# Values as weights in batch 0, and heads 2 to 7 of the second attention block ordered behind the first MoE's start

## The chip, the cores and the metric

The kernel runs on one core of a Trainium2 chip. The metric is the device time of one execution in microseconds (us), as a median over executions. The profile is one such execution taken by the hardware profiler. Engines: TensorE (PE; its weight loads are shown apart as PEld), VectorE (DVE), ScalarE (ACT), GpSimd (POOL), and SyncE (SP), which issues most DMAs.

## What is computed

An attention with decay (4 batches, 8 heads, 576 positions, 64 elements a head), whose output, 2304 tokens of 512, goes through two MoE layers:

```python
scores = scale * np.matmul(q, k.transpose(0, 1, 3, 2))
cum = np.cumsum(np.log(np.clip(f, 0.0001, 1.0)), axis=-1)
decay = cum[:, :, :, None] - cum[:, :, None, :]
scores = np.where(causal, -1000000000.0, scores + decay)
attn = np.exp(scores - np.max(scores, axis=-1, keepdims=True))
attn = attn / (np.sum(attn, axis=-1, keepdims=True) + 1e-09)
x = heads_side_by_side(np.matmul(attn, v))         # [2304, 512]
h = x @ w_in                                       # 512 -> 2048
x = np.maximum(0.01 * h, h) @ w_out                # -> 512
out = ((x @ w_a) * (x @ w_b)) @ w_out2             # 512 -> 1536 -> 512
```

## The kernel before

**The MoE layers** hold most of the work. A MoE operand is kept as a high and a low part (`xh`, `xl`; the same for weights), and each product is done three times: high by high, high by low, low by high. The weights come from DRAM as doubles, 512 KB twice per weight tile, and are turned into the two parts by four VectorE operations in `from_double` (L95, L96, L97, L100), one more for the low part (L88), and two on ScalarE. There are 16 such tiles in the first MoE. Its first stage, `l1` (L594), takes a chunk of 256 tokens and a pair of weight tiles and makes 24 products (L606) into the PSUM tile `h`; `l2` (L621) makes the second stage (products at L633, tile `y`).

**The attention** goes by blocks (b, r): batch b, and r = 0 for queries 0 to 255, r = 1 for 256 to 575. The 64 last queries of a batch are handled apart (`att_last`). Block (0,0) gives chunk 0 of the tokens, which the first MoE products need, and block (0,1) gives chunk 1. Within a block, heads go in pairs, and each head passes through two generators:

- `att_scores` (L192): loads queries and keys, transposes them on TensorE (`tq`, `tk`, in batch 0), makes the mask with the decay on GpSimd into `p` (from the broadcast `cumb`, L336 and L363), the scores on TensorE (`s`), adds and takes the minimum on VectorE (L346), and exponentials on ScalarE with their row sums (`stat`). In batch 0 the scores of both heads of a pair are computed side by side, in the two row halves of the array. In the other batches `p` is then multiplied by the reciprocal of its row sum on ScalarE (L353 to L356).
- `att_values` (L403): transposes `p` (tile `pp`), copies it to SBUF (`ph`), and multiplies by the values. In batch 0 a block of `ph` (128 keys by 128 queries) is the weight and 64 columns of values stream through it, so the result `av` has queries on partitions; VectorE multiplies it by the reciprocal sums (`rec`, `xn`), two transposes (`px`) bring it to the layout of x, and `evac` (L398) splits it: ScalarE copies the high part, VectorE subtracts for the low part.

In block (0,0) `av` and `px` use the PSUM bank with tag `h`, which `l1` uses also. Mask tiles have the tags `p0` and `p1` with two buffers each, so a mask for a later head waits until an earlier `p` has been transposed.

**What sets the order.** The program is written as generators that are interleaved; a planner then simulates the program and orders the instructions of each engine by priority, with an offset of 300 for the attention's engines (class `Ahead`, `pe_att` and its like). The engines run the order as planned. In the main part (L800 on), the attention of batch 0's block (0,0) is issued with a weight tile loaded every nine steps, the first two `l1`/`l2` items of chunk 0 get a priority offset of 2000, and then block (0,1) runs among the remaining items of chunk 0, and items of chunk 1 follow.

Of the kernel before, what the change touches and what calls it, by code (L numbers as in the profile page):

```python
# [8 lines left out]
F32 = mybir.dt.float32  # L9
# [4 lines left out]
ALU = mybir.AluOpType  # L14
# [3 lines left out]
P = 128  # L18
# [8 lines left out]
def kernel(  # L27
# [13 lines left out]
    nc = tc.nc  # L41
# [23 lines left out]
    class Ahead:  # L65
# [5 lines left out]
        def __getattr__(self, name):  # L71
# [5 lines left out]

            return call if self.offset else method

    pe_att, act_att, dve_att, pool_att = (Ahead(e) for e in (nc.tensor, nc.scalar, nc.vector, nc.gpsimd))  # L80

    def f32(ap):
        return ap.bitcast(F32)
# [107 lines left out]

    def att_scores(b, r, h, st):  # L192

        hp, j = h // 2, h % 2
        bh = b * H + h
        a = j * 64
# [127 lines left out]
        for i in range(2):  # L324
# [25 lines left out]
            yield  # L350
            exp(pt, s)
            yield
        if b:  # L353
            rec = over(2 * j, 2)
            for i in range(2):
                act_att.mul(ps[i], ps[i], rec[:, i : i + 1])  # L356
            yield
        if r == 1:
            if j == 0:
                p4s[b, hp] = ap_.tile([P, S], F32, tag="p4", name=f"p4_{nm}")  # L360
# [36 lines left out]

    def evac(hi, lo, src):  # L398
        act_att.copy(hi, src)
        dve_att.tensor_tensor(out=lo, in0=src, in1=f32(hi), op=ALU.subtract)  # L400


    def att_values(b, r, h, st):  # L403
# [44 lines left out]
        for z, (tiles, hi) in enumerate(parts):  # L448
            pp = ps_a.tile([P, 4, P], F32, tag="ps", bufs=3, name=f"pp_{nm}_{z}")
            for m, (kt, i) in enumerate(tiles):  # L450
                pe_att.transpose(pp[:, m, :], ps[i][:, kt * P : kt * P + P], ident)
            if b == 0:
                act_att.copy(hi, pp[:, : len(tiles), :])
            else:
                lo = pl[:, : 3 + z, z, :] if r else pl.rearrange("p a b c -> p (a b) c")[:, 0:3, :]
                evac(hi, lo, pp[:, : len(tiles), :])
            yield
# [4 lines left out]
        if b == 0:  # L462
            if j == 0:
                return

            rec = ap_.tile([P, 4], F32, tag="rec", bufs=3, name=f"rec_{nm}")
            dve_att.tensor_scalar(rec, stats[pair][:, 1, 0:4], 1e-9, None, op0=ALU.add)
            dve_att.reciprocal(rec, rec)
            if r == 0:
                av = ps_y.tile([P, 2, 2, 64], F32, tag="h", bufs=1, name=f"av_{nm}")  # L470
            else:
                av = ps_a.tile([P, 2, 2, 64], F32, tag="ps", bufs=3, name=f"av_{nm}")
            for u in range(2):
                for i in range(2):
                    nt = 2 * r + i + 1
                    for kt in range(nt):
                        pe_att.matmul(av[:, u, i, :], phs[u][:, at[kt, i], :], vhl[:, kt, u, :], start=(kt == 0), stop=(kt == nt - 1))
            xs = ap_.tile([P, 2, 2, 64], F32, tag="xn", bufs=1, name=f"xn_{nm}")
            for u in range(2):
                over_u = rec[:, 2 * u : 2 * u + 2].rearrange("p (i o) -> p i o", o=1).to_broadcast([P, 2, 64])  # L480
                dve_att.tensor_tensor(out=xs[:, :, u, :], in0=av[:, u, :, :], in1=over_u, op=ALU.mult)
            yield
            if r == 0:
                px = ps_y.tile([P, T1], F32, tag="h", bufs=1, name=f"px_{nm}")
            else:
                px = ps_a.tile([P, T1], F32, tag="ps", bufs=3, name=f"px_{nm}")
            for i in range(2):
                pe_att.transpose(px[:, i * P : i * P + P], xs[:, i, :, :].rearrange("p u d -> p (u d)"), ident)
            ch, cl = x_chunk(tok0 // T1)
            evac(ch[:, hp, :], cl[:, hp, :], px)  # L490
            yield
            return
        av = ps_a.tile([P, 256], F32, tag="ps", bufs=3, name=f"av_{nm}")
# [101 lines left out]
    def l1(i, pr):  # L595
        ch, cl = x_chunk(i)
        last = i >= NB1 - 2
        hps = (pools["ps_ab"] if last else ps_y).tile(
            [P, 2, T1], F32, tag="ab0" if last else "h", bufs=2 if last else 1, name=f"h_{i}_{pr}"
        )  # L600
        for u in range(2):
            wih, wil = wa[2 * pr + u][0], wa[2 * pr + u][1]
            n = 0
            for c in reversed(range(ND)):
                for w, x in ((wih, ch), (wih, cl), (wil, ch)):
                    nc.tensor.matmul(  # L606
                        hps[:, u, :], w[:, c * P : c * P + P], x[:, c, :], start=(n == 0), stop=(n == 3 * ND - 1)
                    )
                    n += 1

        hs = mp.tile([P, 2, T1], F32, tag="hs", name=f"hs_{i}_{pr}")
        gh = mp.tile([P, 2, T1], F32R, tag="gh", name=f"gh_{i}_{pr}")
        gl = mp.tile([P, 2, T1], F32R, tag="gl", name=f"gl_{i}_{pr}")
        with tc.high_priority(offset=1):
            nc.scalar.activation(gh, hps, AF.Prelu, alpha=0.01)  # L615
            nc.scalar.activation(hs, hps, AF.Prelu, alpha=0.01)  # L616
        with tc.high_priority(offset=400 if last else 0):
            nc.vector.tensor_tensor(out=gl, in0=hs, in1=f32(gh), op=ALU.subtract)  # L618
        return gh, gl
# [290 lines left out]
```

## Time and profile before

| | us |
|---|---|
| median of 3 runs | 1097.92 (1096.82 to 1098.43) |
| the profiled execution | 1095.32 |
| its span | 1093.5 |
| PE busy in the span | 1064.4 (97%) |
| DVE, ACT, POOL busy | 589.3, 534.6, 216.0 |

The profiled execution has 1.8 us outside its span. On the page, a chain of what ended last is made up of PE for 88%, DVE for 6% and DMA for 3%. Its slices show that DMA is heavily used in the first 60 us and that the clock granted to TensorE is at full speed in nearly all slices.

How to read it: a row of a timeline has the start, the time from there to the end of the last of its records, the engine, the line, the operation, output and inputs by the program's names, shape and count. TensorE's records overlap and their ends are modelled, so what a step takes there is read from start to next start. The line is L76 for all that goes through the class `Ahead`, so such rows are told apart by their names.

### The profile page before, as it was taken

The numbers are of one execution on the slowest core, as the hardware profiler recorded it, in microseconds if no ns is written. First come the engines' busy times: TensorE is split into PE (matmuls) and PEld (weight loads), VectorE is DVE, ScalarE is ACT, GpSimd is POOL, SyncE is SP. The second block draws the span as 40 slices with busy tenths as digits, with TensorE's granted clock in tenths as the row PEclk, the third lists the DMA queues.
The fourth block names the chain that finished last, engine by engine and source line by source line (L and its number), as shares of the span: only waits on it lengthen the run. The fifth ranks groups of instructions, "written<-read, shape, count | busy, mean of one in ns | idle before, by whom it ended". The sixth has DMA issues, their size and how long they took to land.

```text
span 1093.5 us, 19240 instructions
## 1 busy us (share of the span) xinstructions
PE 1064.4 (97%) x7021; PEld 962.3 (88%) x7021; DVE 589.3 (54%) x1314; ACT 534.6 (49%) x1189; POOL 216.0 (20%) x434
## 2 busy tenths in 40 slices
PE   3899999999999999999999999999999999999998
PEld 2678899999999999999999998888888888888897
DVE  5989847868778887577348888212111211211122
ACT  5666658887778788778435554212112111211121
POOL 3834423334233423332000000102002000100000
PEclk9999999999999999999999999999999999999999
DMA  8986135332452435421126562102000100100010
GB/s 234 263 241 185 37 61 110 83 77 61 78 118 62 99 66 98 95 52 43 53 70 206 180 220 82 40 1 77 1 1 25 43 1 1 49 1 1 1 39 21
DMA packets 185727, 86.76 MB, mean 79 GB/s; under 512 B 143840, under 2 KB 173536, under 8 KB 185632
## 3 DMA queue, kind: packets, MB, share of 16 engines
q1 hardware_dynamic: 180736, 80.80, 28.4%
q10 hardware_dynamic: 4896, 4.72, 1.3%
q8 instruction: 56, 0.92, 0.3%
q14 instruction: 39, 0.32, 0.1%
HBM read 75.96 MB, written 9.51 MB: 78 GB/s over the span
## 4 chain that ended last, share of the span: by engine, by line
PE 88%; DVE 6%; DMA 3%; ACT 1%; issue 1%; SPq 1%; POOL 0%; DVEq 0%; POOLq 0%; ACTq 0%
PE ab L702 27%; PE y L633 17%; PE h L606 17%; PE o L725 13%; PE av L76 5%; PE s L76 5%; PE pp L76 3%; DVE w_a L88 1%; DMA raw_a<-in_moe_w_out_dram 1%; DVE c_a L100 1%; DVE c_a L97 1%; DVE c_a L95 1%; DMA cumb<-cum_dram 1%; DVE c_a L96 0%; DVE p L346 0%
## 5 line engine op out<-in xcount | busy, mean ns | idle before, releaser
L702 PE MATMUL ab<-yh,w_ab 128*128 128x512 f32 (+1 forms) x960 | 279.6, 367 | 0.0
L633 PE MATMUL y<-gh,w_a 128*128 128x256 f32 x1152 | 224.8, 282 | 0.0
L606 PE MATMUL h<-xh,w_a 128*128 128x256 f32 x1152 | 224.2, 282 | 0.0
L702 PEld LDWEIGHTS ab<-yh,w_ab 128*128 128x128 f32 x960 | 174.3, 188 | 30.2
L708 DVE TENSOR_TENSOR p<-ab,p 128x512 f32<-128x512 f32 (+1 forms) x60 | 38.3, 638 | 285.1 <-PE ab L702 285.1
L606 PEld LDWEIGHTS h<-xh,w_a 128*128 128x128 f32 x1152 | 183.8, 189 | 3.1 <-issue 1.9
L633 PEld LDWEIGHTS y<-gh,w_a 128*128 128x128 f32 x1152 | 183.3, 188 | 1.0 <-ACT gh L615 0.2
L702 PE MATMUL ab<-yl,w_ab 128*128 128x512 f32 (+1 forms) x480 | 176.4, 367 | 0.0
L606 PE MATMUL h<-xl,w_a 128*128 128x256 f32 x576 | 163.2, 283 | 0.0
L633 PE MATMUL y<-gl,w_a 128*128 128x256 f32 x576 | 161.5, 282 | 0.0
L725 PE MATMUL o<-w_c,pph 128*128 128x512 f32 x432 | 142.6, 390 | 0.0
L707 ACT COPY p<-ab 128x512 f32<-128x512 f32 (+1 forms) x60 | 32.7, 544 | 173.7 <-PE ab L702 173.6
L633 PEld LDWEIGHTS y<-gl,w_a 128*128 128x128 f32 x576 | 108.7, 189 | 2.3 <-issue 1.3
L606 PEld LDWEIGHTS h<-xl,w_a 128*128 128x128 f32 x576 | 108.8, 189 | 1.6 <-issue 1.2
L702 PEld LDWEIGHTS ab<-yl,w_ab 128*128 128x128 f32 x480 | 90.2, 188 | 15.4
L336 POOL TENSOR_SCALAR p<-cumb,ncum_t 128x384 f32<-128x384 f32 (+1 forms) x112 | 77.3, 698 | 128.4 <-PE pp L76 50.4
L87 ACT CAST pph<-p 128x512 fp32r<-128x512 f32 (+1 forms) x60 | 34.7, 578 | 127.6 <-DVE p L708 127.6
L88 POOL TENSOR_TENSOR yl<-sy,yh 128x512 fp32r<-128x512 f32 (+1 forms) x16 | 19.9, 1253 | 389.3 <-ACT yh L87 389.2
L725 PEld LDWEIGHTS o<-w_c,pph 128*128 128x128 f32 x432 | 81.2, 188 | 16.5
L314 ACT ACTIVATE p<-p,stat 128x384 f32<-128x384 f32 (+4 forms) x128 | 76.9, 602 | 37.4 <-DVE stat L346 29.9
L725 PE MATMUL o<-w_c,ppl 128*128 128x512 f32 x216 | 84.3, 390 | 0.0
L618 DVE TENSOR_TENSOR gl<-hs,gh 128x512 fp32r<-128x512 f32 x72 | 51.0, 708 | 41.3 <-ACT hs L616 41.0
(140 smaller groups left out, 1730.9 us busy)
## 6 DMA issues: line engine op xcount, KB each, us to landing
cumb<-cum_dram SPq DMA_DIRECT2D x32, 288.0 KB, 3.8
raw_a<-in_moe_w_in_dram SPq DMA_DIRECT2D x16, 512.0 KB, 4.5
raw_a<-in_moe_w_out_dram SPq DMA_DIRECT2D x16, 512.0 KB, 5.4
raw_ab<-in_moe_w_a_dram SPq DMA_DIRECT2D x12, 512.0 KB, 4.9
raw_ab<-in_moe_w_b_dram SPq DMA_DIRECT2D x12, 512.0 KB, 6.7
raw_c<-in_moe_w_out_dram SPq DMA_DIRECT2D x12, 512.0 KB, 5.9
xq<-in_q_dram SPq DMA_DIRECT2D x144, 32.0 KB, 2.0
y_dram<-yo ACTq DMA_DIRECT2D x18, 256.0 KB, 3.0
```

The costliest lines, as they stand in the source:

```text
L76: return method(*args, **kw)
L87: nc.scalar.copy(hi, src)
L88: (lo_engine or nc.gpsimd).tensor_tensor(out=lo, in0=src, in1=f32(hi), op=ALU.subtract)
L314: act_att.activation(pt, pt, AF.Exp, bias=stat[:, 0, s : s + 1], scale=-1.0, accum_out=stat[:, 1, s : s + 1])
L336: pool_att.tensor_scalar(pt, cumb[:, :n], 1.0, ncum_t[:, t, bh : bh + 1], op0=ALU.mult, op1=ALU.add)
L606: nc.tensor.matmul(hps[:, u, :], w[:, c * P : c * P + P], x[:, c, :], start=(n == 0), stop=(n == 3 * ND - 1))
L618: nc.vector.tensor_tensor(out=gl, in0=hs, in1=f32(gh), op=ALU.subtract)
L633: nc.tensor.matmul(o, w[:, d * P : d * P + P], g[:, u, :], start=(fi == 0 and n == 0 and d % 2 == 0), stop=(fi == NF1 - 1 and n == 2 and d ...
L702: nc.tensor.matmul(o[:, :tn], w[:, c * P : c * P + P], y[:, c, :tn], start=(m == 0), stop=(m == 3 * ND - 1))
L707: nc.scalar.copy(p[:, :tn], ab[0][:, :tn])
L708: nc.vector.tensor_tensor(out=p[:, :tn], in0=ab[1][:, :tn], in1=p[:, :tn], op=ALU.mult)
L725: nc.tensor.matmul(o, g[:, t * P : t * P + P], w, start=(fi == 0 and m == 0), stop=(fi == NF2 - 1 and m == 2))
```

## The change

**Values as weights.** In batch 0, `p` is now multiplied by the reciprocal of its row sum on ScalarE, as in the other batches, by a `rec` for each head. The values of a head (128 keys by 64 elements) are then the weight, and the probabilities stream through it, 256 columns at a time (128 in the last key tile). The two heads of a pair write PSUM partitions 0 to 63 and 64 to 127 of one tile, that is, they use the two column halves of the array; the first product of the pair waits for the copy of the second head's `ph`. The result is in the layout of x as it is, so the multiplication and the transposes `px` go, and `evac` reads `av`. For a pair of block (0,1), 14 products of 64 columns become 6 of 256 and 2 of 128; in block (0,0), 6 become 2 and 2.

**The order.** A class `Behind` adds to each TensorE and VectorE instruction of `att_scores` for heads 2 to 7 of block (0,1) a dependence that is for order alone. On TensorE it stands behind the first `l1` item's 24th product, on VectorE behind the last low part of chunk 0.

```diff
+    class Behind:
+        def __init__(self, engine):
+            self.engine, self.first = engine, None
+        def __getattr__(self, name):
+            method = getattr(self.engine, name)
+            def call(*args, **kw):
+                made = method(*args, **kw)
+                tc.add_manual_dep(made.ins, self.first.ins.name, ORDER, reason="second block behind the first MoE's start")
+                return made
+            return call
+    ORDER = mybir.DependencyInfo(mybir.DependencyClass.NoSync, mybir.DependencyReason.DATA)
...
+    pe_free, dve_free = pe_att, dve_att
+    pe_held, dve_held = Behind(pe_free), Behind(dve_free)
+    def engines_of(b, r, h):
+        return (pe_held, dve_held) if (b, r) == (0, 1) and h >= 2 else (pe_free, dve_free)
...
     def att_scores(b, r, h, st):
+        pe_att, dve_att = engines_of(b, r, h)
...
-        if b:
-            rec = over(2 * j, 2)
-            for i in range(2):
-                act_att.mul(ps[i], ps[i], rec[:, i : i + 1])
-            yield
+        rec = over(2 * j, 2)
+        for i in range(2):
+            act_att.mul(ps[i], ps[i], rec[:, i : i + 1])
+        yield
...
-                act_att.copy(hi, pp[:, : len(tiles), :])
+                st["second"] = act_att.copy(hi, pp[:, : len(tiles), :])
...
-            rec = ap_.tile([P, 4], F32, tag="rec", bufs=3, name=f"rec_{nm}")
-            dve_att.tensor_scalar(rec, stats[pair][:, 1, 0:4], 1e-9, None, op0=ALU.add)
-            dve_att.reciprocal(rec, rec)
...
-            for u in range(2):
-                for i in range(2):
-                    nt = 2 * r + i + 1
-                    for kt in range(nt):
-                        pe_att.matmul(av[:, u, i, :], phs[u][:, at[kt, i], :], vhl[:, kt, u, :], start=(kt == 0), stop=(kt == nt - 1))
-            xs = ap_.tile([P, 2, 2, 64], F32, tag="xn", bufs=1, name=f"xn_{nm}")
-            for u in range(2):
-                over_u = rec[:, 2 * u : 2 * u + 2].rearrange("p (i o) -> p i o", o=1).to_broadcast([P, 2, 64])
-                dve_att.tensor_tensor(out=xs[:, :, u, :], in0=av[:, u, :, :], in1=over_u, op=ALU.mult)
...
-            for i in range(2):
-                pe_att.transpose(px[:, i * P : i * P + P], xs[:, i, :, :].rearrange("p u d -> p (u d)"), ident)
-            ch, cl = x_chunk(tok0 // T1)
-            evac(ch[:, hp, :], cl[:, hp, :], px)
+            nkt = 2 * r + 2
+            for kt in range(nkt):
+                i0 = 1 if kt == nkt - 1 else 0
+                a0 = at[kt, i0]
+                for u in range(2):
+                    made = pe_att.matmul(
+                        av[u * 64 : u * 64 + 64, i0 * P : 256], vhl[:, kt, u, :], phs[u][:, a0 : a0 + 2 - i0, :],
+                        start=(kt == 0), stop=(kt == nkt - 1),
+                    )
+                    if kt == u == 0:
+                        tc.add_manual_dep(made.ins, st["second"].ins.name, SYNC, reason="both heads at once")
+            ch, cl = x_chunk(tok0 // T1)
+            low = evac(ch[:, hp, :], cl[:, hp, :], av)
+            if r == 0:
+                dve_held.first = low
...
+                    if pe_held.first is None and u == 1 and n == 3 * ND - 1:
+                        pe_held.first = made
```

The places where the order changes are shown in three pieces. In the names, a zero for batch 0 is left out at the front: `p_1_0_2` is the mask of block (0,1), head 0, query tile 2; `p_0_6` is head 6 of block (0,0); `h_0` is the first MoE's first pair of weight tiles for chunk 0. The line numbers after the change are 18 to 24 higher.

TensorE just ahead of the first MoE product, before:

```order
L76 MATMUL pp_1_0_0_846<-ident,p_1_0_2_655 128x128 x3
L76 MATMUL px_0_7_531<-ident,xn_0_7_516 128x128 x2
L76 MATMUL tq_1_4_864<-ident,xq_1_4_854 128x128 x2
L76 MATMUL tq_1_4_864<-ident,xk_1_4_855 128x64
L76 MATMUL tk_1_4_0_869<-ident,xk_1_4_855 128x128 x2
L76 MATMUL tk_1_4_2_873<-ident,xk_1_4_855 128x128 x2
L76 MATMUL tk_1_4_2_873<-ident,xk_1_4_855 128x64
L76 MATMUL s_0_1_0_0_738<-kn_1_0_626,qn_1_0_625 64x288
L76 MATMUL s_0_1_0_0_738<-kn_1_0_626,qn_1_0_625 128x288
L76 MATMUL pp_1_0_1_883<-ident,p_1_0_3_703 128x128 x4
L76 MATMUL pp_1_1_0_900<-ident,p_1_1_2_664 128x128 x3
L606 MATMUL h_0_536<-xh_290,w_a_199 128x256
```

And after:

```order
L76 MATMUL av_0_7_525<-ph_0_6_501,vn_0_6_498 64x256
L76 MATMUL av_0_7_525<-ph_0_7_519,vn_0_6_498 64x256
L76 MATMUL av_0_7_525<-ph_0_6_501,vn_0_6_498 64x128
L76 MATMUL av_0_7_525<-ph_0_7_519,vn_0_6_498 64x128
L76 MATMUL tk_1_0_2_642<-ident,xk_1_0_624 128x128 x2
L76 MATMUL tk_1_0_2_642<-ident,xk_1_0_624 128x64
L76 MATMUL s_1_0_2_656<-kn_1_0_622,qn_1_0_621 128x384 x2
L624 MATMUL h_0_532<-xh_288,w_a_195 128x256
L624 MATMUL h_0_532<-xl_289,w_a_195 128x256
```

The transposes `px` are gone, and the transposes of heads 2 to 5, the 512 and 288 scores of heads 0 and 1 and the transposes of their probabilities stand behind the first MoE item.

VectorE up to the last low part of chunk 0 (`xl`), before:

```order
L76 TENSOR_TENSOR xn_0_7_516<-av_0_7_509,rec_0_7_506 128x2x64 x2
L96 TENSOR_SCALAR c_a_720<-c_a_720 128x1024
L88 TENSOR_TENSOR w_a_525<-c_a_519,w_a_525 128x1024
L97 SCALAR_TENSOR_TENSOR c_a_720<-raw_a_482,c_a_720 128x1024
L95 TENSOR_SCALAR c_a_778<-c_a_778 128x1024
L346 ISA p_1_0_3_703,stat_1_0_624<-s_1_0_3_708,p_1_0_3_703 128x512
L346 ISA stat_1_0_624 128x1
L346 ISA p_1_1_3_712,stat_1_0_624<-s_1_0_3_708,p_1_1_3_712 128x512
L346 ISA stat_1_0_624 128x1
L100 SCALAR_TENSOR_TENSOR c_a_720<-raw_a_482,c_a_720 128x1024
L96 TENSOR_SCALAR c_a_778<-c_a_778 128x1024
L76 TENSOR_TENSOR xl_291<-px_0_7_531,xh_290 128x256
```

And after:

```order
L76 TENSOR_TENSOR xl_289<-av_0_5_480,xh_288 128x256
L124 SCALAR_TENSOR_TENSOR c_a_462<-raw_a_377,c_a_462 128x1024
L119 TENSOR_SCALAR c_a_507<-c_a_507 128x1024
L120 TENSOR_SCALAR c_a_507<-c_a_507 128x1024
L112 TENSOR_TENSOR w_a_468<-c_a_462,w_a_468 128x1024
L121 SCALAR_TENSOR_TENSOR c_a_507<-raw_a_428,c_a_507 128x1024
L76 TENSOR_TENSOR xl_289<-av_0_7_525,xh_288 128x256
L371 ISA p_1_0_2_651,stat_1_0_620<-s_1_0_2_656,p_1_0_2_651 128x384
L371 ISA stat_1_0_620 128x1
```

Eight weight steps (41 before the last low part, 33 after), the scores of heads 0 and 1 of block (0,1) and the multiplications `xn` no longer stand ahead of it.

GpSimd at the last masks of block (0,0), before:

```order
L76 AFFINE_SELECT p_0_6_402<-p_0_6_402 128x128
L76 TENSOR_SCALAR p_0_7_414<-cumb_0_6_346,ncum_t 128x128
L76 TENSOR_SCALAR p_0_7_414<-cumb_0_6_346,ncum_t 128x256
L76 AFFINE_SELECT p_0_6_402<-p_0_6_402 128x128
L363 TENSOR_SCALAR p_0_1_0_732<-cumb_1_0_651,ncum_t_71 64x576
L76 AFFINE_SELECT p_0_7_414<-p_0_7_414 128x128 x2
L367 AFFINE_SELECT p_0_1_0_732<-p_0_1_0_732 64x64
```

And after:

```order
L76 TENSOR_SCALAR p_0_6_410<-cumb_0_6_355,ncum_t 128x256
L387 TENSOR_SCALAR p_0_1_0_738<-cumb_1_0_647,ncum_t_71 64x576
L76 AFFINE_SELECT p_0_6_410<-p_0_6_410 128x128
L76 TENSOR_SCALAR p_0_7_434<-cumb_0_6_355,ncum_t 128x128
L76 TENSOR_SCALAR p_0_7_434<-cumb_0_6_355,ncum_t 128x256
L76 AFFINE_SELECT p_0_6_410<-p_0_6_410 128x128
L391 AFFINE_SELECT p_0_1_0_738<-p_0_1_0_738 64x64
```

The first mask row of block (0,1) (64 rows for the last queries, from `cumb_1_0`) has moved from behind both masks of head 7 and the selects of head 6 to a place ahead of them.

## Rows read from the trace of the kernel before

**Rows 1.** Page: busy us (share of the span) x instructions, by engine.
```profile
PE 1064.4 (97%) x7021; PEld 962.3 (88%) x7021; DVE 589.3 (54%) x1314; ACT 534.6 (49%) x1189; POOL 216.0 (20%) x434
```
**Rows 2.** Stretches: us, PE, PEld, DVE, ACT, POOL busy (x), PEclk, DMA, GB/s.
```profile
0.00:70.00 70.00, 46.62 (x185) 32.21 (x186) 56.43 (x111) 42.44 (x90) 35.66 (x55) 0.98 0.88 255
70.00:160.00 90.00, 89.18 (x669) 76.68 (x668) 71.77 (x162) 57.21 (x124) 34.10 (x48) 1.00 0.43 108
67.00:70.00 3.00, 3.00 (x14) 2.79 (x14) 3.00 (x5) 2.17 (x4) 1.49 (x1) 0.50 0.98 334
```
**Rows 3.** Timeline of DVE: start, us, operation, [idle before it, its releaser].
```profile
60.07 0.49 DVE L76 TENSOR_TENSOR xn<-av,rec 128x128 f32<-128x128 f32 x2 [1.97 <-PE av L76]
...
64.34 0.67 DVE L346 CUSTOM_DVE_ANT_0 p<-s,p 128x512 f32<-128x512 f32 x1
...
65.56 1.22 DVE L100 SCALAR_TENSOR_TENSOR c_a<-raw_a,c_a 128x1024 int32<-128x1024 int32 x1
66.69 0.68 DVE L96 TENSOR_SCALAR c_a<-c_a 128x1024 int32<-128x1024 int32 x1
67.30 0.41 DVE L76 TENSOR_TENSOR xl<-px,xh 128x256 fp32r<-128x256 f32 x1
...
124.98 1.28 DVE L88 TENSOR_TENSOR w_a<-c_a,w_a 128x1024 fp32r<-128x1024 f32 x1 [1.17 <-ACT w_a L87]
```
**Rows 4.** Timeline of PE around the first MoE item.
```profile
68.62 0.56 PE L606 MATMUL h<-xh,w_a 128*128 128x256 f32 x1
68.98 0.41 PE L606 MATMUL h<-xl,w_a 128*128 128x256 f32 x1
69.19 0.63 PE L606 MATMUL h<-xh,w_a 128*128 128x256 f32 x2
...
72.29 1.38 PE L76 MATMUL s<-kn,qn 64*64 64x288 f32 x4
73.59 0.44 PE L76 MATMUL pp<-ident,p 128*128 128x128 f32 x2
```
**Rows 5.** Timeline of PE: last weight pair of chunk 0, values, first product of chunk 1.
```profile
146.16 0.28 PE L606 MATMUL h<-xh,w_a 128*128 128x256 f32 x1
146.27 0.28 PE L606 MATMUL h<-xl,w_a 128*128 128x256 f32 x1
...
146.91 3.29 PE L76 MATMUL av<-vn,ph 128*128 128x64 f32 x28
150.01 0.37 PE L76 MATMUL s<-ks,qhh 128*128 128x256 f32 x1
...
157.30 0.28 PE L606 MATMUL h<-xh,w_a 128*128 128x256 f32 x1
```
**Rows 6.** Timeline of PE: scores of both heads of a pair.
```profile
79.01 0.92 PE L76 MATMUL s<-kn,qn 64*128 64x384 f32 x4
...
86.71 1.13 PE L76 MATMUL s<-kn,qn 64*128 64x512 f32 x4 [0.34 <-DVE stat L346]
87.77 0.50 PE L606 MATMUL h<-xh,w_a 128*128 128x256 f32 x2
...
103.27 0.92 PE L76 MATMUL s<-kn,qn 64*128 64x384 f32 x4
104.12 0.39 PE L633 MATMUL y<-gl,w_a 128*128 128x256 f32 x1
```
**Rows 7.** Timeline of PE: the two transposes of one pair's result.
```profile
89.63 0.38 PE L76 MATMUL px<-ident,xn 128*128 128x128 f32 x2
89.84 0.71 PE L76 MATMUL pp<-ident,p 128*128 128x128 f32 x5
```
**Rows 8.** Groups on ACT by form, 0 to 200 us: busy, mean ns | idle before.
```profile
L356 ACT ACTIVATE p<-p,rec 128x256 f32<-128x256 f32 x8 | 4.0, 498 | 0.0
L356 ACT ACTIVATE p<-p,rec 128x128 f32<-128x128 f32 x8 | 3.2, 398 | 3.5 <-DVE rec L320 3.5
```
**Rows 9.** Timeline of POOL: a mask row of block (0,1).
```profile
41.66 1.28 POOL L363 TENSOR_SCALAR p<-cumb,ncum_t 64x576 f32<-64x576 f32 x1 [1.48 <-DMA cumb<-cum_dram]
```

More of the change, by code (lines that the diff above doesn't have):

```diff
@@ L399, in evac @@
         act_att.copy(hi, src)
-        dve_att.tensor_tensor(out=lo, in0=src, in1=f32(hi), op=ALU.subtract)
+        return dve_att.tensor_tensor(out=lo, in0=src, in1=f32(hi), op=ALU.subtract)
     def att_values(b, r, h, st):
@@ L464, in att_values @@
                 return
-            rec = ap_.tile([P, 4], F32, tag="rec", bufs=3, name=f"rec_{nm}")
-            dve_att.tensor_scalar(rec, stats[pair][:, 1, 0:4], 1e-9, None, op0=ALU.add)
-            dve_att.reciprocal(rec, rec)
             if r == 0:
-                av = ps_y.tile([P, 2, 2, 64], F32, tag="h", bufs=1, name=f"av_{nm}")
+                av = ps_y.tile([P, T1], F32, tag="h", bufs=1, name=f"av_{nm}")
             else:
-                av = ps_a.tile([P, 2, 2, 64], F32, tag="ps", bufs=3, name=f"av_{nm}")
@@ L482, in att_values @@
-            yield
-            if r == 0:
-                px = ps_y.tile([P, T1], F32, tag="h", bufs=1, name=f"px_{nm}")
-            else:
-                px = ps_a.tile([P, T1], F32, tag="ps", bufs=3, name=f"px_{nm}")
-            for i in range(2):
-                pe_att.transpose(px[:, i * P : i * P + P], xs[:, i, :, :].rearrange("p u d -> p (u d)"), ident)
-            ch, cl = x_chunk(tok0 // T1)
-            evac(ch[:, hp, :], cl[:, hp, :], px)
+                av = ps_a.tile([P, T1], F32, tag="ps", bufs=3, name=f"av_{nm}")
@@ L605, in l1 @@
                 for w, x in ((wih, ch), (wih, cl), (wil, ch)):
-                    nc.tensor.matmul(
+                    made = nc.tensor.matmul(
                         hps[:, u, :], w[:, c * P : c * P + P], x[:, c, :], start=(n == 0), stop=(n == 3 * ND - 1)
                     )
+                    if pe_held.first is None and u == 1 and n == 3 * ND - 1:
+                        pe_held.first = made
                     n += 1
```

## The prediction, made blind

> **What bounds the kernel now.** I read the busy table of the page first, then the busy times and the granted clock by stretch, then the timelines of VectorE and TensorE around the first MoE. TensorE is busy for 97% of the span [rows 1], but not evenly: 46.62 of the first 70 us against 89.18 of the 90 us after them, and nothing of the change reaches beyond 160 us except by moving the rest earlier [rows 2]. So two things are worth time: the first MoE product comes sooner, or TensorE gets less to do once it is full. Time taken from another engine after 70 us is worth nothing by itself.
>
> What sets the first product is VectorE, busy in nearly all of the time up to 70 us. The last low part of the first chunk of x starts at 67.30; ahead of it VectorE waits 1.97 us for the values product of block (0,0), and converts weights that are needed much later [rows 3]. The first MoE product starts at 68.62, 1.32 us behind that low part [rows 4]. The weights themselves are no limit there: the last of the sixteen is ready at 126.3 and is wanted first at 146.16, a slack of 20 us [rows 3, 5].
>
> **Part 1: values as weights.** Per pair of heads in block (0,1) the old form takes 3.10 us for the values (146.91 to 150.01, 28 records) and 0.21 for the two transposes of the result, 3.31 together [rows 5, 7]. The new form has four passes per pair, three of 256 columns and one of 128, each with both heads in column halves. No row of before shows column halves. The nearest are score pairs, two heads at once in row halves: 0.85 us for 384 columns (103.27 to 104.12), 1.06 for 512 (86.71 to 87.77), so 1.64 ns a column and 0.22 beside the columns [rows 6]. By these a pass of 256 costs 0.64 and one of 128 costs 0.43, 2.35 a pair; if all of the 0.22 hides, as the weight loads of whole-array products do (a new weight every 0.11 us [rows 5]), it is 1.47. Below that I see nothing, since the columns have to stream. I take the middle, 1.9, being between a shape that is like it and a load pattern that is like it: 1.4 saved a pair, 5.6 for four pairs, with 3.8 and 7.4 as ends. In block (0,0) the same edit saves time on an engine that is idle for a third of that stretch [rows 2], so nothing there.
>
> A rule speaks against the better end. The Trainium skill, "TensorE: Matmul & The Clock Gate", Part 3 (What overlaps and what doesn't), says that a weight load runs beside a product in flight only where their row groups differ; column halves share all rows, so by it every load would be bare, and the pair would cost the 2.35. The rows of whole-array products do not agree as they stand (a load for each product, and none of it is seen), so I don't go all the way to that end; by the rule the total below would be 1092.9 in place of 1091.1.
>
> What is added for it: two scalings of the probabilities per head on ScalarE. Like shapes take 0.398 us for 128 columns and 0.498 for 256 [rows 8], 0.78 ns a column, so 0.60 and 0.70 for 384 and 512: 2.6 a pair, 10.4 in block (0,1). ScalarE is busy 57.21 of the 90 us from 70 to 160 [rows 2], so they have room; but they lie between the exponential and the transposes that free the mask's buffer, which is a rival below. VectorE loses two multiplications a pair (0.41 for both: the row's 0.49 less the 0.08 by which durations there run past the next start, 1.22 against the 1.13 from 65.56 to 66.69 [rows 3]) and gains two operations on two columns.
>
> **Part 2: the order.** Rows of the order ahead of the last low part that are now behind it, on VectorE: eight weight steps, four of 0.61 and four of about 1.13, 7.0 us; the scores of heads 0 and 1 of block (0,1), 1.22 for both of 512 columns and by their width 0.92 for both of 384, 2.1; the multiplications of four pairs, 1.6, gone through part 1; and the wait of 1.97, whose cause was a second run through TensorE and back [rows 3]. Eight more operations on two columns come in, by the multiplications of 128 columns at most 0.20 each, 1.6, and at least nothing; 0.6 taken, as nearly all columns are gone. That is 12.1 us sooner, 55.2 for the low part, if nothing else holds it.
>
> Something else may. On GpSimd the order puts a mask row of block (0,1) ahead of the last masks of block (0,0), and that row needs a broadcast which SyncE now issues behind the loads of the next heads. In before such a row waited 1.48 us for its broadcast and took 1.28 [rows 9]: 2.8 us, which I charge in full (its ends are 0 and rival 2 below), so the low part comes at about 58.0 and the first product 1.3 later, at 59.3: 9.3 us sooner than 68.62.
>
> TensorE doesn't win all of that, since it did other work while it waited. Behind the first product now, and ahead of it before, are the 512 scores (1.06 [rows 6]), the 288 scores (1.30, 72.29 to 73.59, whose like stood there [rows 4]), 16 transposes for heads 2 to 5 and 10 of probabilities (26, the narrow ones counted whole, at 0.105 [rows 7], 2.7): 5.1 us. And the first 24 products may run at the lower of the clock's two levels, 1.2 of 2.4 GHz. The clock stood there from 67 to 70 us (granted 0.50), behind a stretch in which TensorE was idle a third of the time, and a product took 0.21 us there [rows 2, 4]; so 24 take 5.1 where the old ones, half of them at the upper level, took 3.6 (68.62 to about 72.2): 1.5 lost. Left of the earlier start: 9.3 - 5.1 - 1.5 = 2.7.
>
> **What comes back.** With TensorE nine microseconds earlier and VectorE's conversions no shorter, the slack of 20 us shrinks, and each conversion, mask and score of block (0,1) is wanted sooner. TensorE waited for VectorE 0.34 us ahead of a score pair in before [rows 6]; I charge some four such waits, 1.5 us, an estimate with 0 and 4 as ends.
>
> **Sum.** 5.6 + 2.7 - 1.5 = 6.8 us. The profiled execution took 1095.32, so 1088.5 by its measure; it lies 2.6 below the median of 1097.92, and I keep that distance: 1091.1. This case alone spreads over 1088 to 1094.5.
>
> **Rivals.**
> 1. Better fed: the mask row and its broadcast hide under the long front, the start keeps its 12.1 (5.5 left after the two deductions), the loads hide (7.4), and no wait comes back: 12.9 saved, 1085.0. For it: the slack of 20 us; against it: VectorE has no idle time in front, so any addition there shows.
> 2. The start comes less early: the masks hold block (0,0) longer than I charge, by 4 us more. 2.8 saved, 1095.1. For it: the mask row waited in before already [rows 9].
> 3. The column halves take turns, so the change doesn't do what it says. The 288 scores do that in before, where the two halves have unlike shapes: 1.30 us, where 288 columns by the slope above would cost 0.69. At the same 1.9 times the pair costs 3.6, a loss of 0.3 a pair: -1.2 + 2.7 - 1.5 = 0, 1097.9. The new code makes the second head's copy a condition of the first product, which should prevent it. The Trainium skill, "TensorEngine Tiling (Array Packing)", Key Properties, lets tiles work independently, but says that a change of tiling mode drains the engine; each pair now switches in and out. No row prices the switch by itself, and it is no part of the sum.
> 4. Slower: the longer pair. A pair of block (0,1) follows the last by 24.3 us (79.01 to 103.27 [rows 6]). Its chain gets two reciprocals and four scalings (2.6 and some hand-overs, 3.5 in all) ahead of the transposes that free its mask buffers, and VectorE's conversions stand among them. If the pair's period sets the end of this stage rather than TensorE's work, all of it shows: 4 times 3.5 is 14 against gains of 8.3, 1103.6. It decides from 2.1 us a pair. Against it: TensorE has MoE products to fill with as long as weights are ready ahead.
>
> **How the numbers follow.** Chances: forecast 0.46, better fed 0.17, later start 0.12, turns 0.14, longer pair 0.11. A measurement of this kernel tells 0.2% from no change, 2.2 us: faster is below 1095.7, slower above 1100.1. Faster: nearly all of the forecast (0.45), all of better fed, and 0.07 of the later start, 0.69. Same: 0.05 of the later start, the turns and 0.01 at the forecast's edge (0.01 of the turns goes over), 0.19. Slower: the longer pair and that 0.01, 0.12. The range 1085.0 to 1099.5 leaves out the longer pair but a sliver, and half of better fed.
>
> **What would show it.** The records of the values product start in pairs a few ns apart, and a pair's eight products take 1.9 us (3.6 would be rival 3; 2.35 bare loads). The last low part of x starts near 58 and the first MoE product near 59 with granted clock 0.5 over its 24; at 55 to 56 it is rival 1, beyond 62 rival 2. The first product of the second chunk, 157.30 in before [rows 5], comes at about 150.5, and from there both kernels run alike. TensorE's waits between 60 and 150 us add up to about 1.5; many waits for probabilities or for VectorE's weights would be rival 4. The forecast is wrong if the first product is early and that first product of the second chunk is not.

## The result, and the profile after

The changed kernel takes 1085.58 us in the median of five runs (1084.52 to 1088.23), the kernel before 1098.15 in five (1096.82 to 1100.24): a ratio of 0.9886, 95% interval 0.987 to 0.9902, so 1.1% faster. The forecast was 1091.1, with 1085.0 to 1099.5 as its range; the time lies at the range's lower end. Measured again beside other kernels, it was 1085.77 (ratio 0.9907, 0.9892 to 0.9921), so the gain is 0.9 to 1.1%.

The spans of the two profiled executions are 1093.5 and 1083.8 us, 9.7 apart. The rest of the 12.6 between the medians is not in the two traces: the profiled execution of before (1095.32) lies below all five runs of it, that of after (1085.58) is at its median. What follows explains the 9.7.

The page after, busy time by engine, answering to [rows 1]:

```profile
PE 1050.4 (97%) x6941; PEld 943.7 (87%) x6941; DVE 588.3 (54%) x1314; ACT 549.2 (51%) x1221; POOL 210.4 (19%) x434
```

TensorE has 14.0 us less to do, ScalarE 14.6 more, VectorE nearly the same. TensorE's timeline at the first MoE item, answering to [rows 4]:

```profile
55.57 1.65 PE L76 MATMUL s<-kn,qn 64*128 64x384 f32 x4 [0.52 <-ACT kn L265]
57.15 0.58 PE L624 MATMUL h<-xh,w_a 128*128 128x256 f32 x1
57.53 0.41 PE L624 MATMUL h<-xl,w_a 128*128 128x256 f32 x1
57.74 0.63 PE L624 MATMUL h<-xh,w_a 128*128 128x256 f32 x2
...
62.17 0.28 PE L624 MATMUL h<-xh,w_a 128*128 128x256 f32 x1
62.28 0.38 PE L76 MATMUL tq<-ident,xq 128*128 128x128 f32 x2
```

The first product starts at 57.15 in place of 68.62, 11.47 us sooner. Its 24 products take 5.13 us (57.15 to 62.28) at 0.21 each, where before they took 3.67, so the item ends 10.01 sooner. The granted clock is 0.50 from 57 to 60 us and 0.65 from 60 to 63, so most of the item ran at the lower of the two levels. VectorE's timeline ahead of it, answering to [rows 3]:

```profile
54.22 1.30 DVE L112 TENSOR_TENSOR w_a<-c_a,w_a 128x1024 fp32r<-128x1024 f32 x1
55.44 1.21 DVE L121 SCALAR_TENSOR_TENSOR c_a<-raw_a,c_a 128x1024 int32<-128x1024 int32 x1
56.57 0.41 DVE L76 TENSOR_TENSOR xl<-av,xh 128x256 fp32r<-128x256 f32 x1
57.38 0.56 DVE L371 CUSTOM_DVE_ANT_0 p<-s,p 128x384 f32<-128x384 f32 x1 [0.39 <-PE s L76]
```

The last low part starts at 56.57, straight behind two weight steps, 10.73 sooner. The values of a pair of block (0,1), answering to the `av` row of [rows 5]:

```profile
88.09 1.73 PE L76 MATMUL av<-ph,vn 128*64 128x256 f32 x16
89.76 0.33 PE L76 MATMUL pp<-ident,p 128*128 128x128 f32 x1
```

A pair takes 1.67 us in place of 3.10 and 0.21. Each of its eight products is two records. In the records the two heads start 7 ns apart (88.094 and 88.101); a record of 256 columns is followed by the next after 0.216 (0.267 for the first), so a product of 256 columns takes 0.43, for both heads at once. The stretch from 70 to 160, answering to [rows 2], and the two scalings and the mask row, answering to [rows 8, 9]:

```profile
70.00:160.00 90.00, 89.67 (x657) 72.43 (x656) 72.45 (x169) 69.52 (x151) 34.54 (x54) 1.00 0.47 125
```
```profile
L380 ACT ACTIVATE p<-p,rec 128x512 f32<-128x512 f32 x10 | 7.1, 709 | 0.0
L380 ACT ACTIVATE p<-p,rec 128x384 f32<-128x384 f32 x10 | 6.1, 614 | 1.4 <-DVE rec L90 1.3
```
```profile
39.12 0.74 POOL L387 TENSOR_SCALAR p<-cumb,ncum_t 64x576 f32<-64x576 f32 x1 [2.72 <-DMA cumb<-cum_dram]
```

**Where the 9.7 us come from.** 10.01 by the end of the first item; less the work that now stands behind it, 5.1 by the prediction's estimate; plus 4 x (3.31 - 1.67) = 6.6 from the values. That would be 11.5. The seventeenth item of 24 products starts at 211.49 in place of 221.26, 9.77 sooner, and the second MoE at 634.93 in place of 644.71, 9.78 sooner. So 1.7 us are missing by 211, and nothing changes after that. They are not waits: from the end of the first item to the seventeenth TensorE has 0.8 us of idle time before and 0.4 after (stretches: us, then PE, PEld, DVE, ACT, POOL busy with counts, granted clock, DMA share, GB/s):

```profile
72.29:221.26 148.97, 148.15 (x1162) 135.22 (x1162) 114.33 (x291) 105.45 (x252) 53.46 (x100) 1.00 0.43 101
62.28:211.49 149.21, 148.76 (x1142) 129.68 (x1140) 122.87 (x305) 120.89 (x281) 54.15 (x105) 1.00 0.50 121
```

Adding up the distances from start to next start by tile in these two stretches shows the sizes. The moved work costs 6.4 us and not 5.1 (16 transposes `tq` and `tk` 2.3, ten `pp` 1.7, the 512 and 288 scores 2.4). The values and `px` save 6.2 and not 6.6, since not every pair of before took 3.10. The scores from `ks`, of the later batches, take 1.3 more and the products into `h` 1.0 less, with the same counts.

### The profile page after: what moved, and what is told of

Read it like the earlier page. It is cut to its first block, busy times and chain, and to the rows that moved or that the text cites. A ratio compares the mean times of both kernels' runs of the same rounds, so it can differ in the third digit from the quotient of the medians.

```text
span 1083.8 us, 19124 instructions
## 1 busy us (share of the span) xinstructions
PE 1050.4 (97%) x6941; PEld 943.7 (87%) x6941; DVE 588.3 (54%) x1314; ACT 549.2 (51%) x1221; POOL 210.4 (19%) x434
## 4 chain that ended last, share of the span: by engine, by line
PE 89%; DMA 4%; issue 2%; ACT 2%; DVE 2%; SPq 1%; POOL 1%; POOLq 0%; ACTq 0%; DVEq 0%
PE ab L722 27%; PE y L653 17%; PE h L624 17%; PE o L745 14%; PE s L76 5%; PE av L76 5%; PE pp L76 4%; DMA raw_a<-in_moe_w_out_dram 1%; DMA cumb<-cum_dram 1%; DMA raw_a<-in_moe_w_in_dram 1%; DMA y_dram<-yo 0%; PE tk L76 0%; ACT p L380 0%; SPq L139 0%; POOL p L361 0%
## 5 line engine op out<-in xcount | busy, mean ns | idle before, releaser
L624 PE MATMUL h<-xh,w_a 128*128 128x256 f32 x1152 | 227.7, 284 | 0.5 <-ACT hs L636 0.3
L361 POOL TENSOR_SCALAR p<-cumb,ncum_t 128x384 f32<-128x384 f32 (+1 forms) x112 | 82.1, 741 | 144.6 <-PE pp L76 70.2
```

The lines of the kernel that those rows point to most:

```text
L361: pool_att.tensor_scalar(pt, cumb[:, :n], 1.0, ncum_t[:, t, bh : bh + 1], op0=ALU.mult, op1=ALU.add)
L624: made = nc.tensor.matmul(hps[:, u, :], w[:, c * P : c * P + P], x[:, c, :], start=(n == 0), stop=(n == 3 * ND - 1))
```

## The experiments

Times are medians; each ratio is to the kernel before on the same chip, where its medians were 1097.21 to 1097.81 (1098.15 in the first measurement). A ratio is not exactly the quotient of two medians. The columns of starts are of TensorE, in each kernel's profiled execution: the first MoE product, the time of its 24, the last weight pair of chunk 0, the first product of chunk 1, the seventeenth item. The last is a mark for kernels whose later work has the same order; where the order changes it can mislead: with one head after the other it is 1.07 later than in the changed kernel, the second MoE 3.89 later (638.82 against 634.93).

| kernel | us | ratio (95%) | first | its 24 | last of chunk 0 | chunk 1 | 17th |
|---|---|---|---|---|---|---|---|
| before | 1098.15 | | 68.62 | 3.67 | 146.16 | 157.30 | 221.26 |
| both parts | 1085.58 | 0.9886 (0.987-0.9902) | 57.15 | 5.13 | 124.07 | 147.53 | 211.49 |
| both, again | 1085.77 | 0.9907 (0.9892-0.9921) | 57.11 | 4.34 | 123.34 | 146.91 | 211.27 |
| values only | 1090.76 | 0.9933 (0.9913-0.9953) | 60.09 | 4.78 | 125.15 | 151.43 | 218.25 |
| order only | 1100.77 | 1.0034 (1.0021-1.0047) | 68.16 | 4.28 | 144.65 | 161.87 | 226.06 |
| one head after the other | 1088.85 | 0.9925 (0.991-0.994) | 57.11 | 4.77 | 125.49 | 150.70 | 212.56 |
| early broadcast | 1086.98 | 0.9908 (0.9894-0.9923) | 56.39 | 3.93 | 121.29 | 147.21 | 212.92 |
| 16 filling transposes | 1095.04 | 0.9984 (0.9973-0.9994) | 62.60 | 4.02 | 128.23 | 154.13 | 219.43 |
| heads 0, 1 held as well | 1094.89 | 0.9983 (0.9974-0.9992) | 57.29 | 5.28 | 117.39 | 157.06 | 219.87 |
| no scaling in (0,1) | 1084.59 | 0.9896 (0.9881-0.991) | 57.33 | 4.86 | 123.98 | 147.41 | 211.39 |
| low parts on GpSimd | 1090.41 | 0.9933 (0.9919-0.9947) | 57.03 | 4.37 | 123.39 | 148.96 | 216.24 |
| the same, early broadcast | 1095.88 | 0.9981 (0.9969-0.9993) | 56.12 | 4.46 | 131.85 | 155.64 | 221.46 |

**The two parts apart.** Values only:

```diff
-        return (pe_held, dve_held) if (b, r) == (0, 1) and h >= 2 else (pe_free, dve_free)
+        return pe_free, dve_free
```

> Only the values part; no instruction of block (0,1) is held back. Theory A: the values part alone takes the multiplications, the second run through TensorE and eight weight steps from ahead of the last low part of x, and the hold moves only eight transposes of heads 2 and 3 on TensorE (nothing on VectorE): first MoE product 57 to 59 us (57.15 with both parts), time 1085.5 to 1088, within 2 us of both parts together. Theory B: the hold carries the earlier start: first product at 62 us or later, time 1090 or more.

Order only, with the old values and no scaling in batch 0:

```diff
-        rec = over(2 * j, 2)
-        for i in range(2):
-            act_att.mul(ps[i], ps[i], rec[:, i : i + 1])
-        yield
+        if b:
+            rec = over(2 * j, 2)
+            for i in range(2):
+                act_att.mul(ps[i], ps[i], rec[:, i : i + 1])
+            yield
...
-            low = evac(ch[:, hp, :], cl[:, hp, :], av)
+            low = evac(ch[:, hp, :], cl[:, hp, :], px)
```

> Only the order part; values computed the old way. Theory A: VectorE still has the same weight steps and the multiplications ahead of the last low part of x, so the first MoE product comes at 66 to 69 us and the time is 1095 to 1099. Theory B (the hold carries the earlier start): first product before 63 us, time 1088 to 1093.

Neither run fits one theory whole: the time of the values alone is that of theory B, their first product (60.09) that of neither; the first product of the order alone (68.16) is that of theory A, its time above both. The values alone bring the time to 1090.76, a good half of the gain; the order alone costs 0.34%. Added up, the two would give 0.3%; together they give 0.9 to 1.1%. So the order's worth depends on the values. TensorE of the values-only kernel shows how the start differs:

```profile
56.06 0.69 PE L76 MATMUL tq<-ident,xq 128*128 128x128 f32 x2
56.68 0.36 PE L76 MATMUL tq<-ident,xk 64*128 64x64 f32 x1
56.97 0.69 PE L76 MATMUL tk<-ident,xk 128*128 128x128 f32 x2
57.59 1.65 PE L76 MATMUL s<-kn,qn 64*128 64x384 f32 x4
59.17 0.98 PE L76 MATMUL tk<-ident,xk 128*128 128x128 f32 x3
60.09 0.58 PE L624 MATMUL h<-xh,w_a 128*128 128x256 f32 x1
```

The low part of x starts at 57.25 here, but TensorE is still at work on the eight transposes of heads 2 and 3, which take 2.45 us (1.53 and 0.92) at the spacing of the lower clock level (the listed clock misses it, see the last section). With the hold they come behind the first item and take 1.12 (62.28 to 63.40) at the upper one. That is 1.3 of the 1.4 us by which the second item is later (66.26 against 64.85). The gap grows to 3.9 us at chunk 1 and 6.8 at the seventeenth item, mostly between 125 and 220 us, where the two kernels' orders differ on all engines. From the end of the first item to the seventeenth TensorE is idle for 3.6 us (busy 149.81 of 153.38), against 0.4 in the changed kernel, so 3.1 us are waits; which difference makes them stays open. The profiled execution is also the slowest of this kernel's four (1092.94; the fastest took 1087.75), so the gap in the trace is larger than in the medians.

In the order-only kernel, x is late whatever TensorE does:

```profile
65.76 2.47 PE L76 MATMUL s<-kn,qn 64*64 64x288 f32 x4 [3.70 <-DVE stat L371]
68.16 0.58 PE L633 MATMUL h<-xh,w_a 128*128 128x256 f32 x1
```

TensorE now waits 3.70 us where it did the second block's transposes before, the first product is 0.46 sooner, and the work that was moved has to be done in the busy stretch: chunk 1 is 4.6 later. The hold on VectorE is not what works: with TensorE's instructions held alone the planner gives the same order on every engine as with both, and with VectorE's alone the same as with none.

**The column halves.** The second head after the first:

```diff
-            for kt in range(nkt):
-                i0 = 1 if kt == nkt - 1 else 0
-                a0 = at[kt, i0]
-                for u in range(2):
+            for u in range(2):
+                for kt in range(nkt):
+                    i0 = 1 if kt == nkt - 1 else 0
+                    a0 = at[kt, i0]
```

> Both parts, but the four passes of the first head come before the four of the second, so that the column halves have no partner. Theory A: the pair's gain is that both halves stream at once: its eight products take 3.0 to 3.6 us in place of 1.67, so the time goes up by 5.3 to 7.7, to 1091 to 1093. Theory B: the gain comes from fewer and longer products whatever runs beside them: the pair stays below 2.2 us, the time within 2 of 1085.6.

```profile
87.69 2.65 PE L76 MATMUL av<-ph,vn 128*64 128x256 f32 x16
90.27 0.33 PE L76 MATMUL pp<-ident,p 128*128 128x128 f32 x1
```

A pair takes 2.58 us, 0.91 more than side by side, 3.6 for four; the time rose by 3.3 (3.1 against the repeated run): between the two theories. So the halves' running at once carries 3.6 of the 6.2 to 6.6, and fewer, longer products and no transposes the rest. The 2.58 is less than expected since the first head's last products run beside the second's first: records of both start at 88.601 and 88.607.

**The mask row that waited.** The broadcast ahead of the pair's loads:

```diff
+        early = (b, r) == (0, 1)
+        if early:
+            cumb = ap_.tile([P, S], F32, tag="cumb", bufs=3, name=f"cumb_{nm}")
+            nc.sync.dma_start(cumb[:, :nk], cum_dram[bh : bh + 1, :nk].to_broadcast([P, nk]))
         if b == 0:
             if j == 0:
...
+        if not early:
...
```

> Both parts, and the broadcast that the first mask row of block (0,1) needs is issued ahead of that pair's loads in place of behind six of them. GpSimd waited 2.72 us for it, and VectorE then 0.95, 1.20 and 0.91 for masks of block (0,0). Theory A: these waits stand on the path to the first product: it comes 1.5 to 3 us sooner (54 to 55.6), time 1082.5 to 1084.5. Theory B: VectorE only does its weight steps at another time and the start stays within 0.7 us of 57.15: time 1085 to 1086.5.

The first product comes 0.76 us sooner, not 1.5 to 3, and the last pair of chunk 0 2.8 sooner (its first 24 products also had more of the upper clock level: granted 0.72 from 57 to 60 us). The wait was not taken away; most of it stands at another place of GpSimd's queue:

```profile
35.16 1.47 POOL L392 TENSOR_SCALAR p<-cumb,ncum_t 64x576 f32<-64x576 f32 x1 [2.29 <-DMA cumb<-cum_dram]
```

VectorE's waits for masks ahead of the last low part fall from 3.06 us (0.95, 1.20 and 0.91) to 1.73. Then the gain is all given back. The chain of this kernel's profile at the change of chunks (start, us, engine, tile):

```profile
139.89 1.26 PE pp L76 x10
141.15 1.36 PE s L76 x4
142.50 0.02 issue
142.53 0.42 ACT qhh L302
...
147.53 0.34 DVE xl L429
147.91 2.02 PE h L629 x15
```

Up to 142.5 the chain is TensorE's own work; then chunk 0 is used up, and the last low part of chunk 1 comes at 147.5, as in the repeated run of the changed kernel (147.51; 148.12 in its first profile). TensorE waits 1.2 us there, where the changed kernel has no idle time between 60 and 147 us. So with this earlier start block (0,1)'s attention sets the second chunk; in the changed kernel itself it doesn't yet. The next run says so more strongly: heads 0 and 1 held as well.

```diff
-        return (pe_held, dve_held) if (b, r) == (0, 1) and h >= 2 else (pe_free, dve_free)
+        return (pe_held, dve_held) if (b, r) == (0, 1) else (pe_free, dve_free)
```

> Both parts, and heads 0 and 1 of block (0,1) are held behind the first 24 products as well, eight more transposes and a score pair that take 4.3 us at the lower clock level before them. Theory A: what is moved from the lower level to the upper is won again (1 to 2 us), as with heads 2 and 3: 1083.5 to 1085. Theory B: the chain of block (0,1)'s pairs now sets the second chunk, and it starts 5 us later: 1087 to 1091, with TensorE waits between 120 and 160 us.

```profile
57.29 0.58 PE L624 MATMUL h<-xh,w_a 128*128 128x256 f32 x1 [3.17 <-DVE xl L76]
62.28:147.53 85.25, 85.25 (x620) 67.75 (x619) 70.58 (x148) 65.84 (x131) 32.77 (x50) 1.00 0.49 136
62.57:157.06 94.49, 90.41 (x639) 70.27 (x638) 76.60 (x172) 73.24 (x155) 24.39 (x50) 1.00 0.46 123
157.06 0.38 PE L624 MATMUL h<-xh,w_a 128*128 128x256 f32 x1 [1.04 <-ACT xh L423]
```

The first row is the start: TensorE is idle for 3.2 us ahead of the first product, and the product still comes at 57.29, since the last low part of chunk 0 (56.82) sets it. The stretches from the end of the first item to chunk 1, the changed kernel's first, then this one's, show what comes after: no idle time there, 4.1 us here, the last 1.04 of it for chunk 1's high part. Chunk 0 is finished 6.7 us sooner (its last pair starts at 117.39) and chunk 1 starts 9.5 later, and the time is 1094.89: theory B, at more than its price. Of the three settings tried (none, heads 2 to 7, all), heads 2 to 7 is the best.

**The scalings.** Left out in block (0,1):

```diff
-        rec = over(2 * j, 2)
+        if (b, r) != (0, 1):
+            rec = over(2 * j, 2)
...
```

> Both parts, but in block (0,1) the probabilities are not scaled (that block's result lacks its normalisation). It measures what the scalings cost: by the prediction's forecast they lie beside other work, within 1 us of the changed kernel. By its rival of the longer pair, 2 to 10 us faster than that, with the first product of the second chunk earlier than 145.5 us.

1084.59 against 1085.77 on the same chip: they cost about 1.2 us, a little over the forecast's 1, and chunk 1 starts at the same time (147.41). The rival of the longer pair, at 2 to 10, falls, although the sum had nothing for the scalings.

**Filling TensorE's idle time.**

```diff
+                if hp == 1 or hp == 2:
+                    bank = ps_y.tile([P, 2, T1], F32, tag="y", bufs=2, name=f"fill_{hp}")
+                    for m in range((0, 12, 4)[hp]):
+                        fill = pe_att.transpose(bank[:, 0, 0:P], ident, ident)
...
```

> Both parts, and 16 transposes of the identity, read by nobody, after the values products of heads 3 and 5 (12 and 4), where TensorE waited 3.11 and 1.1 us. Theory A: the lower clock level at the first MoE products (0.21 us a product until 62.1) comes from these idle stretches: the first 24 products take 2.8 to 4.2 us in place of 5.13 and the time falls by 1 to 2.5. Theory B: so few do nothing for the clock: the 24 take 4.9 to 5.3 and the time stays within 0.7, or rises by up to 1 where a transpose stands in the way.

The 24 took 4.02, but without any filling they took 4.34 in the repeated run and 3.93 with the early broadcast, so this tells nothing of the clock. The time was lost elsewhere:

```profile
48.53 1.55 PE L76 MATMUL av<-ph,vn 128*64 128x256 f32 x8 [3.33 <-ACT ph L76]
50.01 1.12 PE L76 MATMUL fill<-ident 128*128 128x128 f32 x4
54.94 1.52 PE L76 MATMUL pp<-ident,p 128*128 128x128 f32 x6 [3.81 <-ACT p L76]
```
```profile
46.67 1.05 ACT L111 CAST w_a<-c_a 128x1024 fp32r<-128x1024 f32 x1 [1.65 <-DVE c_a L124]
47.62 0.85 ACT L76 COPY ph<-pp 128x384 f32<-128x384 f32 x2
```

The planner put weight steps ahead of the attention's copies on ScalarE, which waited for VectorE there (1.65, and 1.50 at 53.04), and the first product came 5.5 us later. In this profile the attention of block (0,0) passes from engine to engine, and a weight step ahead of its copies on ScalarE holds it up; a run with that order alone was not made.

**Relief for VectorE.** The low parts of weight tiles 8, 10, 12 and 14 on GpSimd, alone and with the early broadcast:

```diff
-    split(w[:, 0, :], w[:, 1, :], t, nc.vector)
+    split(w[:, 0, :], w[:, 1, :], t, nc.gpsimd if name in ('a_8', 'a_10', 'a_12', 'a_14') else nc.vector)
```

> Both parts, and the low parts of four weight tiles (8, 10, 12, 14) are subtracted on GpSimd in place of VectorE, some 4.9 us of VectorE's time between 60 and 125 us. Theory A: with both parts in, the chunk-0 products run out at 140 us and the second chunk waits for block (0,1)'s chain, which VectorE's queue lengthens; it comes earlier by 1 to 3 us and the time is 1082.5 to 1084.5. Theory B: the chain waits for GpSimd's masks as much as for VectorE, and the weights' low parts now stand among them: no gain, 1085 to 1088.

> The same with the early broadcast of block (0,1), whose 2 to 3 us at the start were given back by 147 us, because the second chunk was not ready. Theory A: the freed VectorE lets the second chunk follow the earlier start, so both gains show: first product at 56.4, the second chunk's at 144 to 146, time 1080.5 to 1083.5. Theory B: the second chunk stays at 147 or later, time 1085 to 1088.

```profile
L112 POOL TENSOR_TENSOR w_a<-c_a,w_a 128x1024 fp32r<-128x1024 f32 x4 | 12.9, 3237 | 9.9 <-ACT w_a L111 7.0 <-PE pp L76 2.8
89.62 3.31 POOL L112 TENSOR_TENSOR w_a<-c_a,w_a 128x1024 fp32r<-128x1024 f32 x1 [1.94 <-ACT w_a L111]
90.72 3.29 DVE L124 SCALAR_TENSOR_TENSOR c_a<-raw_a,c_a 128x1024 int32<-128x1024 int32 x1
```

No gain, as in theory B, at a higher price: one subtraction takes 3.24 us on GpSimd (1.22 on VectorE), and GpSimd waits 9.9 us ahead of the four, 7.0 of it for their high parts, with the masks queued behind. And VectorE was not relieved. Beside each of the four subtractions one of its steps ran long: 2.67 in place of 0.69, and 3.29, 2.19 and 2.18 in place of 1.22. That is 6.0 us more, against the 4.9 that were moved away; VectorE is busy for 63.43 of the 65 us from 60 to 125, against 62.28 in the changed kernel. TensorE is idle for 4.2 us from the end of the first item to the seventeenth, against 0.4. With the early broadcast it is worse. No version that computes the whole result was faster than the changed kernel; the yardstick run:

> The changed kernel once more, as a yardstick on the same chip for the other runs of this group: 0.987 to 0.990 of the kernel before; first MoE product at 57.1 us, first product of the second chunk at 147.5.

Its first product came in as expected (57.11), its ratio of 0.9907 a little above the 0.987 to 0.990 expected, and its chunk 1 at 146.91, 0.6 us sooner.

## Why the prediction was right, step by step

The sign and its two sources held: an earlier start and less work on TensorE, with nothing changed after 160 us but by shifting. The time was 5.5 us below the forecast and 0.6 inside the range. It lies nearer to rival 1's number (1085.0, given 0.17) than to the forecast, and only in part for its reasons.

- **Values: 1.9 us a pair predicted, 1.67 measured**, so 6.6 saved by the prediction's own rows (6.2 by all records) and not 5.6. The step that was off is the middle between bare and hidden loads: the loads hide. A product of 256 columns takes 0.43 us, two records 0.216 apart with a weight load for each, where the row halves of the scores suggested 0.64 with 0.22 beside the columns and 0.42 without. The pair lies 0.2 above the 1.47 of hidden loads, most of it at its two ends (0.267 in place of 0.216 behind the first record, 0.203 in place of 0.109 behind the last). The rule of the Trainium skill, "TensorE: Matmul & The Clock Gate", Part 3 (What overlaps and what doesn't), that loads overlap with products in flight only across row groups, does not hold for these column halves: the loads share all rows with the products in flight, and no time is seen for them. By it, the pair would have been 2.35, an estimate from the row halves.
- **Column halves in turn (rival 3)**: excluded by the 7 ns between the heads, and by the 3.3 us that it costs to part them. The product ahead of a pair takes 0.21 to the pair's start instead of 0.12, and the pair's last record 0.20 instead of 0.11. What the Trainium skill, "TensorEngine Tiling (Array Packing)", Key Properties, says of a drain on a change of mode is therefore small here, 0.2 us a pair if all of that is the drain.
- **Start: 59.3 predicted, 57.15 measured.** The wait of the mask row was there as named (2.72 us for the broadcast), but the step that charged it in full was wrong: the low part came at 56.57, between the 55.2 without any charge and the 58.0 with it. VectorE did weight steps in a part of the time, which it had to do anyway. How much of the wait reached the start stays open, since the early broadcast left 2.29 of it and moved the first product by 0.76. The rest of the miss is the 1.3 from the low part to the first product, which was 0.58 here. In before, TensorE still had transposes to do there, seven of them from 67.22 to 68.62:

```profile
67.22 1.75 PE L76 MATMUL pp<-ident,p 128*128 128x128 f32 x7
```

- **The first item at the lower level: 5.1 predicted, 5.13 measured** in this profile. So close a hit is luck: the repeated run of the same kernel has 4.34, and the kernels of the experiments 3.9 to 5.3.
- **What comes back: 1.5 predicted, 1.7 measured**, and here the number is luck and the mechanism wrong. The prediction charged waits for VectorE; TensorE's listed waits after 57 us are 0.3, and it is idle for less than before. What came back is TensorE's own work, chiefly the moved work, which costs 6.4 and not the 5.1 taken from narrow rows. The second chunk limits a kernel only once the start is sooner or more is held back, as the early broadcast and the wider hold showed. The prediction did not name that; its nearest was rival 4, whose cause, the scalings, is worth 1.2.
- **Sum by the traces: 6.8 predicted, 9.8 measured**; 3.0 short, 1.0 from the values and 2.2 from the start, less 0.2 that came back more. Keeping the distance of 2.6 between profiled execution and median was the other miss: the profiled execution of after is at its median. The two, 2.9 in the profiled executions and 2.6, make up the 5.5 between forecast and time.
- **What the prediction took as two additive parts** was one: the order part, which it priced with the values part in one walk through VectorE's queue, loses time by itself. The walk gave the joint effect to within 2.2 us, and so could not show that the hold on VectorE does nothing.

## What to carry to other kernels

Work that is put behind a start pays only if the start can come sooner by another change; otherwise it leaves the idle time that hid it and lands in the busy stretch. A wait on one engine need not reach the start, since the engines behind it may do work meanwhile that has to be done anyway. The test is to move the suspected wait, to see in the trace how much of it is left, and to look at the first product. Price moved work at what it costs beside its new neighbours: the walk through narrow rows was 1.3 us short. When a stage starts sooner, ask what the next stage waits for, since the one further gain at the start here was given back by the second chunk.

## What was not expected of the hardware

- Products of 64 columns of weights stream in the two column halves at once, a record of 256 columns of both heads every 0.216 us and two records a product, with no time seen for the weight loads: 1.67 us a pair. The same work with the probabilities as weights took 3.10.
- The granted clock as listed can miss the lower level. In the values-only profile it says 1.00 from 40 to 70 us, while the products go at 0.21 us, the spacing of the lower level, until 64 us. The spacing of like products is the surer sign.
- A subtraction of 128 x 1024 takes 3.24 us on GpSimd and 1.22 on VectorE, and a step of VectorE beside it can run as long. The same kind of step is slowed or not by where it stands: without the early broadcast L124 went from 1.26 to 1.69 us on average and L121 stayed at 1.26, with it L121 went from 1.25 to 1.71 and L124 stayed at 1.28:

```profile
L124 DVE SCALAR_TENSOR_TENSOR c_a<-raw_a,c_a 128x1024 int32<-128x1024 int32 x9 | 15.2, 1693 | 0.1
L121 DVE SCALAR_TENSOR_TENSOR c_a<-raw_a,c_a 128x1024 int32<-128x1024 int32 x9 | 15.4, 1708 | 0.1
```

Why a step beside a subtraction on GpSimd is held up was not tested.
